# Two heads on alternate partitions: one transpose and one masked copy for both head groups

## The chip, the cores and the metric

The kernel runs on one core of a Trainium2 chip. The metric is the device time of one execution in microseconds. A core has TensorE (PE, matmuls, with its weight loads shown as PEld), VectorE (DVE), ScalarE (ACT), GpSimd (POOL), the queue that issues stores (SP) and 16 DMA engines. PE reads SBUF and writes PSUM.

## The reference

Inputs q, k, v are float32 of shape 8 x 8 x 576 x 64 (batch, head, token, width). The first half is attention inside chunks of 64 tokens, the second mixes the tokens of a batch:

```python
scores = 1/sqrt(64) * q_c @ k_c.T          # per chunk of 64 tokens
attn   = softmax(scores)
x      = (attn @ v_c), heads side by side  # 8 x 576 x 512
wq, wk = x @ w_q, x @ w_k                  # 576 x 64 each
mixed  = 1/sqrt(64) * (wq @ wk.T) @ x
out    = relu(mixed) @ w_out               # 576 x 512, float32
```

## The kernel before

**Order.** The whole program is a list of words, ORDER (L18), one for each step; the loop at L404 turns each into instructions. Each engine takes its own instructions in the order of the list, and semaphores join the engines. A word names the step, the batch, a part, and where it matters a PSUM bank (`@4`) or the engine that does the copy (`:A` ACT, `:D` DVE, `:P` POOL). All work of the eight batches is interleaved in that list; there is no loop over batches.

**Loads.** LD (L115) loads a batch with POOL's DMA queue, which casts float32 to float16 on the way. q and k come in two transfers each, one for each group of four heads (g = 0, 1): partition (head, run) holds a run of 18 tokens, so 4 heads x 32 runs fill 128 partitions, with 18 x 64 elements in each (L137). v comes in four transfers to 32 partitions each (L117). CP (L144) moves half of v 32 partitions up, so that pairs of chunks stand under one another; POOL does it 27 times.

**Transposes.** TR (L172) turns q or k of one head group with DVE, in blocks of 32 x 32 words. A word is two float16 values (the pair of widths 2d, 2d+1). From a block, 32 partitions with the runs of one head, each partition afterwards holds the width pair, and the tokens lie along it as "x r": the 32 values of one block come to stand 18 words apart in q, 9 words apart in k, whose tokens are also split into two halves `e`. q goes to qT, k to kN.

**Masked copies.** The two heads that share 64 rows are kept apart by zeros. MK (L182) copies kN to kT, multiplied by a column `mask` that is 1 on the rows of one head (hp = 0 or 1) and 0 on the others, with separate instructions for even and odd chunks (5 and 4 of them): 2 groups x 2 heads x 2 = 8 instructions a batch.

**Scores to output.** SC (L192) multiplies kT as weights with qT, two matmuls for each pair of words (the even and the odd width, `e`), on the upper and the lower 64 rows at once; both operands are read with a step of 2 float16. EX (L206) takes the exponential on ACT, PV (L220) multiplies with v and a column of ones, RN (L251) divides on DVE. XT and XE (L262, L270) transpose the result on PE and copy it out of PSUM, PJ and EP (L277, L299) give wq and wk, DU (L302) puts a second copy of wq on the other rows, WT and EW (L305, L313) transpose wk, GM and EG (L320, L334) build G = wk.T @ x, MX and RL (L337, L349) multiply wq with G and take the relu, OM and OE (L374, L386) multiply with w_out and copy to the staging tile, which lies over the q and k of batches already used. Stores go through SP's queue; the first two wait until the last two loads have landed (L476).

**Zeros.** ZZ (L400) is a matmul of zeros, 128 x 128 x 512, whose result nobody reads. The order has 48 of them, all but one before the work of batch 2.

Of the kernel before, what the change touches and what calls it, by code (L numbers as in the profile page):

```python
# [23 lines left out]
XE0.0:A RN0.2 XT0.1@0 XE0.1:A ZZ@4 ZZ@5 ZZ@2 ZZ@3 ZZ@6 ZZ@4 PJ0@0 EP0:A TR1.1 TR1.0 MK1.0:D MK1.1:D SC1.0@4 WT0@0
EX1.0 TR1.3 EW0:D TR2.0 CL3 DU0:D TR1.2 MK1.2:A GM0@0 ZZ@7 ZZ@2 PV1.0@2 RN1.0 EG0:A MX0.2@0 MX0.3@6 MK1.3:A RL0.2:A
RL0.3:A TR2.1 MK2.1:D SC1.1@4 EX1.1 SC1.2@0 MX0.0@6 RL0.0:A ZZ@2 ZZ@3 ZZ@2 MX0.1@2 EX1.2 RL0.1:A PV1.1@4 PV1.2@0 ZZ@6
RN1.1 MK2.0:A OM1@6 XT1.0@7 RN1.2 OM2@4 XT1.1@0 XE1.0:D TR2.3 MK2.2:D MK2.3:D TR2.2 LD3.k0 LD3.k1 CP2.0:P LD3.v0
LD3.v1 LD4.k0 CP2.2:P LD3.q1 LD3.v2 LD4.k1 LD3.v3 CP3.0:P CP3.1:P LD4.v0 LD4.q1 LD4.q0 LD5.k0 CP3.2:P LD4.v2 LD4.v1
CP3.3:P SC2.0@2 OM0@7 OE1:A CP2.1:A XE1.1:A EX2.0 OE2:A PJ1@0 PV2.0@2 RN2.0 CP2.3:D TR3.0 EP1:A WT1@6 SC2.1@0 SC2.2@4
DU1:A EW1:A EX2.1 GM1@6 PV2.1@0 RN2.1 EX2.2 EG1:A OE0:A MX1.0@4 MX1.1@2 RL1.0:A RL1.1:A MX1.3@6 PV2.2@4 MX1.2@0  # L30
RL1.3:A RL1.2:A TR3.1 RN2.2 OM4@2 OM6@3 XT2.0@0 MK3.0:A XT2.1@4 TR3.3 MK3.1:D MK3.3:D MK3.2:D TR4.1 ZZ@6 TR3.2 OM5@1
SC3.0@6 OE4:A XE2.0:A XE2.1:A OE5:A EX3.0 PJ2@4 EP2:A OE6:A OM8@1 WT2@0 SC3.1@4 SC3.2@2 OE8:A EW2:A EX3.1 PV3.0@6
EX3.2 GM2@0 PV3.1@4 EG2:A MK4.1:A MK4.0:D TR4.3 RN3.0 OM7@2 OE7:A RN3.1 DU2:P LD5.q0 CP4.0:P LD4.v3 PV3.2@6 MX2.2@0
RL2.2:A MX2.1@4 RL2.1:A MK4.2:D RN3.2 TR4.0 MK4.3:D TR5.1 TR4.2 XT3.0@3 XE3.0:A MX2.0@0 OM3@2 RL2.0:A MX2.3@6 RL2.3:A
XT3.1@4 XE3.1:A LD5.q1 LD5.v1 LD5.k1 LD6.q0 LD5.v3 CP4.1:P CP4.2:P LD5.v0 CP4.3:P LD5.v2 CP5.1:P LD6.k0 LD6.v1 LD6.v3
LD6.k1 LD7.v0 LD6.v2 LD6.q1 LD6.v0 CP5.0:P CP5.2:P CP5.3:P LD7.k0 SC4.0@0 OM9@3 PJ3@4 EX4.0 OE9:A EP3:A OE3:A PV4.0@0
SC4.1@6 EX4.1 WT3@4 OM10@5 SC4.2@2 EW3:A EX4.2 MK5.0:D TR5.0 DU3:D RN4.0 PV4.1@6 RN4.1 GM3@4 PV4.2@0 RN4.2 OM11@2
MK5.1:A EG3:A OE10:A MX3.0@6 MX3.1@3 XT4.0@5 OE11:A RL3.0:A RL3.1:A XT4.1@0 SC5.0@6 MX3.2@2 TR5.3 XE4.0:D MK5.3:D
MK5.2:D TR5.2 XE4.1:A OM13@4 RL3.2:A EX5.0 PJ4@0 MX3.3@2 OM12@5 EP4:A RL3.3:A OE13:A OE12:A SC5.1@0 EX5.1 SC5.2@2
WT4@4 PV5.0@6 EX5.2 EW4:A TR6.0 TR6.1 RN5.0 OM16@5 PV5.1@0 RN5.1 PV5.2@2 GM4@4 RN5.2 OM15@6 XT5.0@7 OE16:A MK6.0:A  # L40
EG4:A MK6.1:D TR6.3 XE5.0:D TR6.2 MK6.3:D MK6.2:D TR7.1 LD7.k1 CP6.1:P LD7.q0 DU4:P LD7.v2 CP7.0:P LD7.v3 CP6.0:P
CP6.3:P LD7.q1 LD7.v1 CP6.2:P MX4.3@4 MX4.1@0 OE15:A RL4.3:A RL4.1:A XT5.1@2 XE5.1:A SC6.0@4 MX4.2@0 OM17@6 EX6.0
PJ5@2 OM14@7 MX4.0@4 OE17:A EP5:A RL4.2:A RL4.0:A WT5@6 EW5:D SC6.1@2 EX6.1 PV6.0@0 SC6.2@4 EX6.2 RN6.0 GM5@6 PV6.1@2
PV6.2@4 RN6.1 RN6.2 DU5:P EG5:A OE14:A MX5.0@0 OM19@6 OM20@7 MK7.1:A RL5.0:A OE19:A OE20:A XT6.0@2 XE6.0:A XT6.1@4
MX5.1@0 RL5.1:A MX5.2@6 TR7.3 XE6.1:D OM18@3 PJ6@4 MK7.3:A EP6:A RL5.2:A OM23@2 TR7.0 MK7.0:D SC7.0@0 WT6@4 MX5.3@6
OE18:A EW6:A CP7.2:P CP7.3:P CP7.1:P DU6:P TR7.2 OE23:D RL5.3:D MK7.2:D EX7.0 OM21@5 GM6@4 PV7.0@0 SC7.2@6 SC7.1@2
OE21:A EG6:A EX7.2 EX7.1 RN7.0 MX6.1@4 OM22@6 RL6.1:D MX6.3@0 PV7.1@2 PV7.2@4 RN7.1 RN7.2 RL6.3:A OE22:A OM26@7
MX6.0@0 OM24@6 RL6.0:A XT7.0@0 XT7.1@4 MX6.2@2 OM25@1 RL6.2:A XE7.0:D XE7.1:D PJ7@4 OM28@0 OE25:A EP7:A WT7@1 OM27@4
# [6 lines left out]
def kernel(  # L55
# [24 lines left out]
    RUN = S // 32  # L80
# [10 lines left out]
    qT = [sb.tile([P, 2, S, 2], F16, name=f"qT{i}") for i in range(2)]  # L91
    kN = sb.tile([P, 2, S, 2], F16, name="kN")
    kT = [sb.tile([P, 2, NCH, 2, CH, 2], F16, name=f"kT{i}") for i in range(2)]
# [21 lines left out]
    def load(b, what):  # L115
        n = int(what[1:]) if what[1:] else -1
        if what[0] == "v":  # L117
            half, f = divmod(n, 2)
            m = slice(NG // 2 * half, NG // 2 * (half + 1))
            src = v[b].rearrange("h (c i e) d -> i (h c) (e d)", i=32, e=2)  # L120
            loads.append(
                nc.gpsimd.dma_start(  # L122
                    vt[b % NVB][CH * f + 32 : CH * f + CH, m, 0 : 2 * D],
                    src[:, NG * half + f : NG * (half + 1) : 2],
                )
            )
            return
        s = "qk".index(what[0])
        if n < 0:
            loads.append(  # L130
                nc.gpsimd.dma_start(
                    qk[b // 2][:, b % 2, s].rearrange("p (g r) d -> p g (r d)", g=2),
                    (q, k)[s][b].rearrange("(g h) (p r) d -> (h p) g (r d)", g=2, r=RUN),
                )
            )
            return
        loads.append(  # L137
            nc.gpsimd.dma_start(  # L138
                qk[b // 2][:, b % 2, s, RUN * n : RUN * n + RUN].rearrange("p r d -> p (r d)"),
                (q, k)[s][b].rearrange("(g h) (p r) d -> g (h p) (r d)", g=2, r=RUN)[n],  # L140
            )
        )

    def pair(b, half, f, eng):  # L144
        m = slice(NG // 2 * half, NG // 2 * (half + 1))
# [24 lines left out]
            )  # L170

    def tr(b, g, s):  # L172
        to = (kN if s else qT[b % 2])[:, g].bitcast(F32).rearrange("p n o -> p (n o)")
        frm = qk[b // 2][:, b % 2, s, RUN * g : RUN * g + RUN].bitcast(F32)
        if s:
            to = to.rearrange("p (e x r) -> p r e x", e=2, r=RUN // 2)
            frm = frm.rearrange("p (r e) x -> p r e x", e=2)
        else:
            to = to.rearrange("p (x r) -> p r x", r=RUN)
        nc.vector.transpose(out=to, in_=frm)  # L180

    def mk(b, g, hp, eng):  # L182
        one = mask[:, hp : hp + 1]
        for odd in range(2):
            dst = kT[b % 2][:, g, odd::2, hp ^ odd].rearrange("p c (e i) o -> p c e (i o)", e=2)
            frm = kN[:, g].rearrange("p (e c i) o -> p c e (i o)", e=2, c=NCH)[:, odd::2]
            if eng == "A":
                nc.scalar.activation(dst, frm, AF.Copy, scale=one)  # L188
            else:
                nc.vector.tensor_scalar(dst, frm, one, None, op0=ALU.mult)  # L190

    def sc(b, u, bank):  # L192
        for i in range(8 if u < 2 else 2):
            g, c = (u, i) if u < 2 else (i, NCH - 1)
            for e in range(2):
                for t in range(2):
                    rows = slice(CH * t, CH * t + CH)
                    nc.tensor.matmul(  # L198
                        ps[:, bank + t, CH * i : CH * i + CH],
                        lhsT=kT[b % 2][rows, g, c, :, :, e].rearrange("p f n -> p (f n)"),  # L200
                        rhs=qT[b % 2][rows, g, CH * c : CH * c + CH, e],
                        start=(e == 0),
                        stop=(e == 1),
                    )
# [199 lines left out]
    for word in ORDER:  # L404
# [107 lines left out]
```

## Time and profile before

| | |
|---|---|
| median of 3 runs | 118.85 us (118.61 to 119.23) |
| profiled execution, its own time | 118.47 us |
| its span, first to last instruction | 116.6 us |
| mean granted clock of PE | 0.985 |

A line of a group view gives line, engine, operation, output and input tile with shape and count, then busy time, mean length of one in ns, and the engine's idle time just ahead of them with what ended it. A line of a timeline gives start, length, engine, line, operation and count; where several instructions are merged, the length is that of the group. One instruction may start while the one before it is in its last stage, so lengths can add up to more than the busy time.

### The profile page before, as it was taken

The numbers are of one execution on the slowest core, as the hardware profiler recorded it, in microseconds if no ns is written. First come the engines' busy times: TensorE is split into PE (matmuls) and PEld (weight loads), VectorE is DVE, ScalarE is ACT, GpSimd is POOL, SyncE is SP. The second block draws the span as 40 slices with busy tenths as digits, with TensorE's granted clock in tenths as the row PEclk, the third lists the DMA queues.
The fourth block names the chain that finished last, engine by engine and source line by source line (L and its number), as shares of the span: only waits on it lengthen the run. The fifth ranks groups of instructions, "written<-read, shape, count | busy, mean of one in ns | idle before, by whom it ended". The sixth has DMA issues, their size and how long they took to land.

```text
span 116.6 us, 4132 instructions
## 1 busy us (share of the span) xinstructions
PE 99.8 (86%) x1768; PEld 55.9 (48%) x1768; DVE 92.4 (79%) x155; ACT 89.5 (77%) x142; POOL 61.9 (53%) x105
## 2 busy tenths in 40 slices
PE   5937998778998799979979979689999979999940
PEld 2403654434665465636644736355654535543410
DVE  2099399999999999999997999998799768515520
ACT  4069907599999999999996998679999982477220
POOL 6958597377679269994769999552500100010000
PEclk9999599999999999999999999999999999999999
DMA  1999999999999999999999999999799986007982
GB/s 11 177 200 177 199 194 211 192 201 203 197 193 204 196 201 186 190 195 194 189 195 165 169 178 200 210 192 129 296 400 415 411 351 280 23 3 304 379 315 88
DMA packets 27202, 24.52 MB, mean 210 GB/s; under 512 B 20784, under 2 KB 20784, under 8 KB 27184
## 3 DMA queue, kind: packets, MB, share of 16 engines
q0 software_dynamic: 24880, 14.82, 90.8%
q1 hardware_dynamic: 2304, 9.44, 20.3%
q8 instruction: 14, 0.23, 0.7%
q14 instruction: 4, 0.03, 0.1%
HBM read 29.62 MB, written 9.44 MB: 335 GB/s over the span
## 4 chain that ended last, share of the span: by engine, by line
DMA 43%; PE 33%; POOL 12%; issue 5%; ACT 2%; DVE 1%; POOLq 0%; DVEq 0%
DMA vt<-in_v_dram 39%; PE pb L378 18%; POOL vt L295 6%; DMA qk<-in_q_dram 4%; POOL vt L122 3%; POOL qk L138 3%; PE pb L341 3%; PE pb L198 3%; PE pb L283 3%; PE pb L266 3%; PE pb L325 2%; PE pb L232 2%; ACT qk L293 1%; DVE xn L255 1%; ACT rmx L356 1%
## 5 line engine op out<-in xcount | busy, mean ns | idle before, releaser
L378 PE MATMUL pb<-wout,rmx 128*128 128x512 f16 x144 | 36.4, 382 | 0.0
L255 DVE TENSOR_TENSOR xn<-pb,rec 128x896 f16<-128x896 f32 (+1 forms) x24 | 25.1, 1047 | 0.8
L295 POOL COPY vt<-vt 32x576 int32<-32x576 int32 x27 | 18.1, 674 | 11.4 <-DMA vt<-in_v_dram 10.7
L122 POOL DMA_DIRECT2D vt<-in_v_dram x32 | 21.8, 687 | 3.4 <-DMA vt<-in_v_dram 1.2
L356 ACT ACTIVATE rmx<-pb 128x576 f16<-128x576 f32 x29 | 18.3, 663 | 5.9 <-PE pb L341 5.7
L180 DVE STREAM_TRANSPOSE kN<-qk 128x576 f32<-128x576 f32 x16 | 19.4, 1213 | 4.0 <-DMA qk<-in_k_dram 4.0
L188 ACT ACTIVATE kT<-kN,mask 128x640 f16<-128x640 f16 (+1 forms) x24 | 17.4, 786 | 5.1 <-DVE kN L180 4.9
L293 ACT COPY qk<-pb 128x512 f32<-128x512 f32 x30 | 17.6, 607 | 4.1 <-PE pb L378 3.9
L180 DVE STREAM_TRANSPOSE qT<-qk 128x576 f32<-128x576 f32 x16 | 19.7, 1243 | 0.1
L208 ACT ACTIVATE est<-pb 128x1024 f16<-128x1024 f32 (+1 forms) x24 | 19.2, 826 | 0.4 <-PE pb L198 0.3
L378 PEld LDWEIGHTS <-rmx 128*128 128x128 f16 x144 | 12.5, 103 | 13.0 <-issue 0.5
L198 PE MATMUL pb<-qT,kT 64*128 64x64 f16 x576 | 13.0, 193 | 4.0 <-ACT kT L188 2.8
L401 PE MATMUL pb<-zz 128*128 128x512 f16 x48 | 14.5, 437 | 1.2 <-DVE zz L423 1.2
L190 DVE TENSOR_SCALAR kT<-kN,mask 128x640 f16<-128x640 f16 (+1 forms) x40 | 14.9, 423 | 0.1
L198 PEld LDWEIGHTS <-kT 64*128 64x128 f16 x576 | 10.8, 96 | 8.1 <-ACT kT L188 4.2
L293 ACT COPY xT<-pb 128x1280 f16<-128x1280 f16 (+1 forms) x10 | 11.4, 1146 | 4.0 <-PE pb L266 3.7
L295 POOL COPY wq<-wqk 64x288 int32<-64x288 int32 x5 | 2.1, 422 | 22.6 <-ACT wqk L293 19.1
L232 PE MATMUL pb<-vt,est 64*64 64x65 f16 x576 | 9.9, 197 | 2.4 <-issue 1.8
L266 PE MATMUL pb<-ident,xn 128*128 128x128 f16 (+1 forms) x160 | 10.9, 214 | 0.4 <-DVE xn L255 0.4
L266 PEld LDWEIGHTS <-xn 128*128 128x128 f16 (+1 forms) x160 | 9.2, 97 | 3.9 <-issue 1.2
L232 PEld LDWEIGHTS <-est 64*64 64x64 f16 x576 | 7.8, 109 | 6.4 <-issue 5.0
L138 POOL DMA_DIRECT2D qk<-in_k_dram x16 | 9.2, 576 | 2.5 <-DMA qk<-in_k_dram 1.1
(40 smaller groups left out, 102.9 us busy)
## 6 DMA issues: line engine op xcount, KB each, us to landing
out_dram<-qk SPq DMA_DIRECT2D x10, 768.0 KB, 6.7
qk<-in_k_dram POOLq DMA_DIRECT2D x16, 288.0 KB, 8.0
qk<-in_q_dram POOLq DMA_DIRECT2D x16, 288.0 KB, 7.9
vt<-in_v_dram POOLq DMA_DIRECT2D x32, 144.0 KB, 7.8
out_dram<-qk SPq DMA_DIRECT2D x6, 256.0 KB, 3.4
wout<-in_moe_w_out_dram POOLq DMA_DIRECT2D x1, 512.0 KB, 9.8
wpj<-in_moe_w_q_dram POOLq DMA_DIRECT2D x1, 64.0 KB, 8.3
wpj<-in_moe_w_k_dram POOLq DMA_DIRECT2D x1, 64.0 KB, 7.6
```

Of the source, the lines that this page charges most:

```text
L122: nc.gpsimd.dma_start(vt[b % NVB][CH * f + 32 : CH * f + CH, m, 0 : 2 * D], src[:, NG * half + f : NG * (half + 1) : 2],)
L180: nc.vector.transpose(out=to, in_=frm)
L188: nc.scalar.activation(dst, frm, AF.Copy, scale=one)
L198: nc.tensor.matmul(ps[:, bank + t, CH * i : CH * i + CH], lhsT=kT[b % 2][rows, g, c, :, :, e].rearrange("p f n -> p (f n)"), rhs=qT[b % 2] ...
L208: nc.scalar.activation(est[b % 2][u].rearrange("p i n c -> p i (n c)"), ps[:, bank : bank + 2, 0:n], AF.Exp, scale=scale_attn,)
L232: nc.tensor.matmul(ps[CH * o : CH * o + CH, bank + hp, VP * m : VP * m + VP], lhsT=est[b % 2][t][rows, i, at], rhs=vt[b % NVB][rows, slot, ...
L255: nc.vector.tensor_tensor(out=xn[b % 2][:, 7 * u : 7 * u + n].rearrange("p m (h d) -> p h m d", h=2), in0=xw[:, :, :, 0:D], in1=rec[u][:, ...
L266: nc.tensor.transpose(t16[:, at % 1024 : at % 1024 + r], xn[b % 2][0:r, n, :], ident[0:r, 0:r])
L293: nc.scalar.copy(dst, src)
L295: nc.gpsimd.tensor_copy(dst.bitcast(I32), src.bitcast(I32))
L356: nc.scalar.activation(dst, src, AF.Relu, scale=scale_moe)
L378: nc.tensor.matmul(ps[:, bank, :], lhsT=c.rearrange("p (t r) -> p r t", r=size)[:, r], rhs=wout[:, i, :], start=(i == 0), stop=(i == NI - 1),)
```

## The change

From batch 1 on, a transfer of q or k still carries one head group, but puts it on every second partition (64 of 128), each with a run of 36 tokens: the two groups then lie on alternate partitions. Batch 0 stays as it was.

One transpose takes both groups. A block of 32 partitions now holds 16 runs of one head from each group, and the two groups' words become neighbours: the tokens lie as "x r g". One masked copy then takes both groups, and even and odd chunks together. For that, kN gets 64 more token places, zeroed once, and kT is laid out in ten chunks of 128 x 2. Scores from batch 1 on read weights and moving side with a step of 4 float16 (2 for batch 0). The last chunk of GM reads 128 rows, of which the upper 64 meet zero weights, and not 64.

The order is a new one. In words that count here: ZZ 48 to 1, TR 32 to 18, MK 32 to 18 (and one instruction for each, not two), MK on ACT 12 to 4 and on DVE 20 to 14; CP on POOL 27 to 22, on ACT 2 to 1, on DVE 3 to 9; DU on POOL 5 to 0, on ACT 1 to 4, on DVE 2 to 4; EP and EG on DVE 0 to 2 each; the second XE on DVE 2 to 4; OE on DVE 6 to 7, RL 3 to 4. The loads of batch 0 start k, k, q, q and not k, q, k, q.

```diff
-            return
-        loads.append(
-            nc.gpsimd.dma_start(
-                qk[b // 2][:, b % 2, s, RUN * n : RUN * n + RUN].rearrange("p r d -> p (r d)"),
-                (q, k)[s][b].rearrange("(g h) (p r) d -> g (h p) (r d)", g=2, r=RUN)[n],
-            )
-        )
+        src = (q, k)[s][b]
+        if b == 0:
+
+            dst = qk[0][:, 0, s, RUN * n : RUN * n + RUN]
+            src = src.rearrange("(g h) (p r) d -> g (h p) (r d)", g=2, r=RUN)[n]
+        else:
+
+            dst = qk[b // 2][n::2, b % 2, s]
+            src = src.rearrange("(g h) (p r) d -> g (h p) (r d)", g=2, r=NG)[n]
+        loads.append(nc.gpsimd.dma_start(dst.rearrange("p r d -> p (r d)"), src))
...
+        elif s:
+            to = to.rearrange("p (e n) -> p e n", e=2)[:, :, 0:S]
+            to = to.rearrange("p e (x r g) -> p r e x g", r=RUN, g=2)
+            frm = frm.rearrange("p (r e) (x g) -> p r e x g", e=2, g=2)
+        else:
+            to = to.rearrange("p (x r g) -> p r x g", r=NG, g=2)
+            frm = frm.rearrange("p r (x g) -> p r x g", g=2)
         nc.vector.transpose(out=to, in_=frm)
...
-        for odd in range(2):
-            dst = kT[b % 2][:, g, odd::2, hp ^ odd].rearrange("p c (e i) o -> p c e (i o)", e=2)
-            frm = kN[:, g].rearrange("p (e c i) o -> p c e (i o)", e=2, c=NCH)[:, odd::2]
...
+        dst = dst.rearrange("p (m j e i) o -> p m j e (i o)", j=4, e=2, i=n)
+        dst = dst[:, :, 1:3] if hp else dst[:, :, 0::3]
+        frm = frm.rearrange("p (e m j i) o -> p m j e (i o)", e=2, j=2, i=n)
...
-                        lhsT=kT[b % 2][rows, g, c, :, :, e].rearrange("p f n -> p (f n)"),
-                        rhs=qT[b % 2][rows, g, CH * c : CH * c + CH, e],
+                        lhsT=kv[rows, g, c, :, e],
+                        rhs=qv[rows, g, CH * c : CH * c + CH, e],
...
-                r = P if j < 4 else CH
...
-                    lhsT=wkn[b % 2][0:r, j, :],
-                    rhs=xn[b % 2][0:r, n, :],
+                    lhsT=wkn[b % 2][:, j, :],
+                    rhs=xn[b % 2][:, n, :],
...
+            pad = kN.bitcast(F32).rearrange("p (e n) o -> p e (n o)", e=4)
+            nc.vector.memset(pad[:, :, S // 2 :], 0.0)
```

More of the change, by code (lines that the diff above doesn't have):

```diff
@@ L24 @@
[L24 to L48, printed above, removed]
@@ L90 @@
     vt = [sb.tile([P, NG, VW], F16, name=f"vt{i}") for i in range(NVB)]
-    qT = [sb.tile([P, 2, S, 2], F16, name=f"qT{i}") for i in range(2)]
-    kN = sb.tile([P, 2, S, 2], F16, name="kN")
-    kT = [sb.tile([P, 2, NCH, 2, CH, 2], F16, name=f"kT{i}") for i in range(2)]
+    qT = [sb.tile([P, 2 * S, 2], F16, name=f"qT{i}") for i in range(2)]
+    SP = S + CH
+    kN = sb.tile([P, 2 * SP, 2], F16, name="kN")
+    kT = [sb.tile([P, 4 * SP, 2], F16, name=f"kT{i}") for i in range(2)]
     mask = sb.tile([P, 2], F32, name="mask")
@@ L183, in mk @@
         one = mask[:, hp : hp + 1]
[L184 to L192 removed]
+        dst, frm, n = kT[b % 2], kN, CH
+        if b == 0:
+            dst, frm, n = dst[:, 2 * SP * g : 2 * SP * g + 2 * SP], frm[:, SP * g : SP * g + SP], CH // 2
+        dst = dst.rearrange("p (m j e i) o -> p m j e (i o)", j=4, e=2, i=n)
+        dst = dst[:, :, 1:3] if hp else dst[:, :, 0::3]
+        frm = frm.rearrange("p (e m j i) o -> p m j e (i o)", e=2, j=2, i=n)
+        if eng == "A":
+            nc.scalar.activation(dst, frm, AF.Copy, scale=one)
+        else:
+            nc.vector.tensor_scalar(dst, frm, one, None, op0=ALU.mult)
+    def sc(b, u, bank):
+        if b == 0:
+            qv = qT[0].rearrange("p (g n) o -> p g n o", g=2)
+            kv = kT[0].rearrange("p (g c m) o -> p g c m o", g=2, c=NCH + 1)
+        else:
+            qv = qT[b % 2].rearrange("p (n g) o -> p g n o", g=2)
+            kv = kT[b % 2].rearrange("p (c m g) o -> p g c m o", c=NCH + 1, g=2)
         for i in range(8 if u < 2 else 2):
```

58 lines of the change are left out of this document (39 added, 19 removed).

## The prediction

> **What bounds the kernel now.** I read the busy shares first, then a table of stretches (columns: stretch and its length, then busy time and instruction count of PE, PE's weight loads, DVE, ACT and POOL, then granted clock, DMA share and GB/s), then the same table for the zero matmuls alone (PE and weight loads only).
>
> ```profile
> span 116.6 us, 4132 instructions
> PE 99.8 (86%) x1768; PEld 55.9 (48%) x1768; DVE 92.4 (79%) x155; ACT 89.5 (77%) x142; POOL 61.9 (53%) x105
> ```
> ```profile
> 0.00:20.00 20.00, 15.61 (x205) 7.81 (x206) 12.55 (x27) 10.55 (x13) 14.98 (x29) 0.91 1.16 166
> 20.00:30.00 10.00, 8.26 (x188) 4.58 (x186) 9.50 (x18) 8.75 (x15) 6.68 (x12) 1.00 1.37 198
> 30.00:80.00 50.00, 44.74 (x916) 27.10 (x915) 48.75 (x79) 46.44 (x75) 37.03 (x60) 1.00 1.37 192
> 80.00:112.20 32.20, 31.22 (x464) 16.44 (x461) 21.63 (x34) 23.27 (x42) 3.24 (x6) 1.00 0.72 276
> 112.20:116.60 4.40, 0.00 (x0) 0.00 (x0) 0.00 (x0) 0.53 (x1) 0.00 (x0) 1.00 0.45 169
> ```
> ```profile
> 0.00:20.00 20.00, 11.72 (x39) 4.04 (x40) 0.91 1.16 166
> 20.00:30.00 10.00, 2.41 (x9) 0.52 (x7) 1.00 1.37 198
> 30.00:80.00 50.00, 0.39 (x1) 0.10 (x1) 1.00 1.37 192
> 80.00:112.20 32.20, 0.00 (x0) 0.00 (x0) 1.00 0.72 276
> ```
>
> The reader is to see three different kernels in one span. From 30 to 80 us DVE is busy 48.75 of 50 us and ACT 46.44: the vector engines set the pace, and PE idles 5.26 us. From 80 to 112.2 PE is busy 31.22 of 32.2 us, with DVE and ACT a third idle: PE works off what it could not do before. Without the zero matmuls PE has 3.89 + 5.85 + 44.35 + 31.22 = 85.3 us of real work. So of the 112.2 us up to its last matmul, PE has no real work in hand for 16.1 us (before 20), 4.15 (20 to 30), 5.65 (30 to 80) and 1.0 (80 to 112.2). Behind that lie 4.4 us of last copy and store. A gain must come out of the 16.1 or out of the 10.8 us after 20.
>
> The loads seem to be a bound too: the rate of the page stands near 195 GB/s until 80 us. The store queue tells when the last loads have landed, because the first store waits for them; the third row is PE's last product with the values of batch 7.
>
> ```profile
> GB/s 11 177 200 177 199 194 211 192 201 203 197 193 204 196 201 186 190 195 194 189 195 165 169 178 200 210 192 129 296 400 415 411 351 280 23 3 304 379 315 88
> 81.63 31.45 SPq L394 DMA_DIRECT2D out_dram<-qk  x16
> 96.51 0.23 PE L232 MATMUL pb<-vt,est 64*64 64x65 f16 x4
> ```
>
> From that product (96.7) to the end is 19.9 us. With loads done at 81.6, and three to four pair copies of 0.7 us (a row below) and the product behind them, the end could be near 105. The loads leave 7 us of room to the span that I forecast.
>
> **The change, part by part.** *Transposes.* The q and k of a batch from 1 on take 2 transposes of 1,152 words instead of 4 of 576: 28 become 14, batch 0 keeps 4. Each group of 32 writes now goes to 16 pairs of neighbouring words instead of 32 single words, 36 or 72 bytes apart.
>
> ```profile
> L180 DVE STREAM_TRANSPOSE qT<-qk 128x576 f32<-128x576 f32 x16 | 19.7, 1243 | 0.1
> L180 DVE STREAM_TRANSPOSE kN<-qk 128x576 f32<-128x576 f32 x16 | 19.4, 1213 | 4.0 <-DMA qk<-in_k_dram 4.0
> L255 DVE TENSOR_TENSOR xn<-pb,rec 128x896 f16<-128x896 f32 x16 | 17.5, 1092 | 0.6
> L255 DVE TENSOR_TENSOR xn<-pb,rec 128x768 f16<-128x768 f32 x8 | 7.7, 958 | 0.3
> ```
> ```profile
> 45.39 1.22 DVE L180 STREAM_TRANSPOSE kN<-qk 128x576 f32<-128x576 f32 x1
> 46.45 1.24 DVE L180 STREAM_TRANSPOSE qT<-qk 128x576 f32<-128x576 f32 x1
> 47.53 1.12 DVE L190 TENSOR_SCALAR kT<-kN,mask 128x640 f16<-128x640 f16 x2
> ```
>
> A transpose holds DVE for 1.07 us (start to start), 1.86 ns a word. The two sizes of L255 differ by 134 ns for 128 elements: DVE passes one in 1.05 ns where nothing hinders it. So the new transpose lies between 1,152 x 1.05 + 0.07 = 1.28 us and 2 x 1.07 - 0.07 = 2.07 us (0.07 for a start: half of the 0.15 that 1,092 ns leave over 896 x 1.05, as neighbours overlap); no transpose of the trace writes neighbours. k (36 bytes apart) and q (72) differ by 30 ns for the same words, so where the writes go does count, and the reads, which are contiguous in both, do not explain the 1.86. I take 1.28. Then the transposes hold DVE for 4 x 1.07 + 14 x 1.28 = 22.2 instead of 34.2 us (-12.0); at 2.07 it would be -0.9.
>
> The Trainium skill (SBUF — State Buffer, "Specifications (TRN2)") has 16-byte lines and asks for two accesses a line for full bandwidth: pairs would pass at full rate, single words not, so by it the sum is the one below. No run here shows it.
>
> *Mask copies.* From batch 1 on 2 instructions per batch with 2,560 elements, in batch 0 4 with 1,280: 18 in all, for 64. DVE gets 12 long and 2 short ones, ACT 2 and 2.
>
> ```profile
> L190 DVE TENSOR_SCALAR kT<-kN,mask 128x640 f16<-128x640 f16 x20 | 8.8, 441 | 0.1
> L190 DVE TENSOR_SCALAR kT<-kN,mask 128x512 f16<-128x512 f16 x20 | 8.1, 406 | 0.0
> L188 ACT ACTIVATE kT<-kN,mask 128x640 f16<-128x640 f16 x12 | 10.1, 844 | 5.1 <-DVE kN L180 4.9
> L188 ACT ACTIVATE kT<-kN,mask 128x512 f16<-128x512 f16 x12 | 8.7, 727 | 0.0
> 65.91 2.50 DVE L190 TENSOR_SCALAR kT<-kN,mask 128x640 f16<-128x640 f16 x4
> 66.17 2.09 POOL L295 COPY vt<-vt 32x576 int32<-32x576 int32 x3
> ```
>
> By the slope of the two sizes (0.273 and 0.914 ns an element) a long one takes 0.97 us on DVE and 2.60 on ACT, a short one 0.62 and 1.43. DVE: 12.8 for 16.9 (-4.1). ACT: 8.1 for 18.8 (-10.7). Beside POOL copies four masks took 2.42 us instead of 1.7: were each long one to wait for one such copy (0.7), DVE would lose 8 us. The means hold such waits already, so I add none.
>
> *What the new order moves.* Counted in the two orders, DVE gets 6 more pair copies, 2 duplicates, 2 projection copies, 2 G copies, 2 xT copies of 1,280, one output copy and one relu.
>
> ```profile
> L297 DVE COPY vt<-vt 32x1152 f16<-32x1152 f16 x3 | 1.4, 453 | 0.7 <-DMA vt<-in_v_dram 0.6
> L297 DVE COPY wq<-wqk 64x576 f16<-64x576 f16 x2 | 0.6, 302 | 0.0
> L358 DVE TENSOR_SCALAR rmx<-pb 128x576 f16<-128x576 f32 x3 | 2.3, 751 | 0.1
> L297 DVE COPY wkn<-pb 128x320 f16<-128x320 f16 x3 | 1.0, 326 | 2.9 <-PE pb L309 2.4 <-ACT rmx L356 0.4
> L297 DVE COPY xT<-pb 128x1280 f16<-128x1280 f16 x2 | 1.6, 812 | 0.0
> L297 DVE COPY qk<-pb 128x512 f32<-128x512 f32 x6 | 4.1, 689 | 4.1 <-PE pb L378 4.1
> ```
>
> 6 x 0.45 + 2 x 0.30 + 2 x 0.75 + 2 x 0.4 (between 0.33 and 0.75) + 2 x 0.81 + 0.69 + 0.75 = +8.7 us, some 3 of it after 80 us where DVE is idle a third. Together DVE goes from 92.4 to 85 (96 with slow transposes). ACT falls to 78.8 by its masks; the xT, projection, G, output and relu copies that DVE takes from it outweigh three more duplicates, so under 79. POOL loses 5 pair copies and 5 duplicates, and its 67 issues stay. The q and k loads past POOL's queue become 64 rows of twice the length; the v loads of the trace fill 32 partitions only and run in the same band of GB/s, so I count no loss.
>
> A new memset of 128 words stands ahead of the first transpose, where DVE waits for its load; without that cover it would cost some 0.1 to 0.2 us.
>
> ```profile
> 5.69 1.21 DVE L180 STREAM_TRANSPOSE kN<-qk 128x576 f32<-128x576 f32 x1 [3.80 <-DMA qk<-in_k_dram]
> ```
>
> *PE.* 47 of 48 zero matmuls go. They lay in time in which PE waited anyway, save part of the 2.41 us after 20; real work stays 85.3, plus 0.3 for the zero that is left. Score reads step 8 bytes instead of 4, in weights and moving side: between nothing and a doubling of 19.5 ns (40 in 0.78 us, below) for 504 matmuls, 9.8 us; I take nothing, since all their reads step already and the nearest change is by one factor of two. G's last chunk reads 128 rows instead of 64 with the same columns: nothing.
>
> *The start.* With the zero matmuls the granted clock was 1.00 but for one stretch:
>
> ```profile
> 10.00:15.00 5.00, 5.00 (x126) 2.77 (x120) 2.92 (x7) 4.46 (x6) 3.51 (x6) 0.66 1.57 193
> 12.16 1.25 PE L198 MATMUL pb<-qT,kT 64*128 64x64 f16 x40
> 47.74 0.78 PE L198 MATMUL pb<-qT,kT 64*128 64x64 f16 x40
> 20.51 1.14 PE L283 MATMUL pb<-xT,wpj 128*128 128x512 f16 x8
> ```
>
> At a clock of 0.66 scores took 1.25 us instead of 0.78, 1.6 times. Without zeros batch 0's steps up to the projection run like that: of 3.2 us on the path (first products, last transposes, projection, next scores) some 1.9 more. k's second half is loaded ahead of q's first, and the first scores come up to 1 us later; two transposes for batch 1 instead of four gain about as much. I take +1.5, between 0 and 3.
>
> **The sum.** Real work 85.6; idle before 20 us 16.1 + 1.5; idle after 20; tail 4.4. The idle after 20 was 10.8. In 30 to 80 us the longest engine was 97.5% busy (48.75 of 50) with the second at 93%; with DVE and ACT shortened PE is the longest there. Kept at 97.5%, its 44.35 us cost 1.1 of idle; at worst 5.65 stays. In 20 to 30 it is 0.3 to 4.15. I take 2.3 and 1.3, nearer the low ends by the 97.5%, and 1.0 after 80: 4.6. Span: 85.6 + 17.6 + 4.6 + 4.4 = 112.2. The profiled execution took 118.47 us, 1.9 above its span, and the median of the runs is 118.85, 0.4 above it: 112.2 + 1.9 + 0.4 = 114.5.
>
> **Rivals.**
> *Transposes stay slow.* The 1.86 ns may belong to the 32 x 32 blocks and not to the writes. For it: no row of neighbouring writes, and the 36- and 72-byte rows differ by 2% only. Then DVE, full from 30 to 80 already, has 96 instead of 92.4: 118.85 + 3.6, about 122.5. It decides from 1.8 us a transpose, where DVE is back at 92.4. Slower; 0.18.
> *The room isn't used.* PE idles 10.8 after 20 us as now, since the new order starves it elsewhere: span 118.4, time 120.7. Against it: the waits of 30 to 80 lie with full DVE and ACT. 0.12.
> *Score reads cost.* Half of the bound of 9.8: 119.4. 0.05.
> *The clock stays low.* If it holds at 0.66 until 30 us, the 5.85 us of work of 20 to 30 takes 1.6 times, 3.5 more: 118. The Trainium skill (TensorE: Matmul & The Clock Gate, "Part 1: The HAM clock gate") has half rate after an idle window of about 3.4 us and full rate after a busy one, which would end this soon after PE is dense; the trace agrees in that the clock is at 1.00 from 15 us on. Faster by a little; 0.05.
> *Everything fits.* Idle at 2.4 after 20, start at no cost: 110.8. 0.12.
>
> **Chances.** Forecast 0.48 (112 to 117.5 as its own range). Within 0.5% (118.3 to 119.4, about what a measurement can tell from no change) only one case falls. Faster: forecast, everything fits and the low clock, 0.65. Within: the score reads, 0.05. Slower: slow transposes and unused room, 0.30. The range takes in everything fits below and the unused room above, 110 to 121.5, and leaves out most of the slow transposes.
>
> **What would show it.** Transposes from batch 1 at 1.2 to 1.4 us each (over 1.8: the first rival); long masks near 0.97 on DVE; DVE's busy time near 85 and ACT's under 79; PE above 95% from 30 us on; 40 scores still in 0.78 us at full clock; clock under 1 before 20 us. The forecast is wrong if PE keeps gaps of 1 us behind DVE or the loads after 30 us, or if the loads land after 89.

## The result and the profile after

| | before | changed |
|---|---|---|
| median of the runs | 118.73 us (118.37 to 119.23) | 150.24 us (149.34 to 150.66) |
| ratio, 95% interval | | 1.264 (1.256 to 1.272) |
| profiled execution's span | 116.6 us | 147.8 us |
| busy PE / DVE / ACT / POOL | 99.8 / 92.4 / 89.5 / 61.9 us | 98.4 / 94.3 / 79.4 / 56.3 us |

The forecast was 114.5 us in a range of 110 to 121.5. The change costs 31.5 us. Medians, here and below, are of all runs of a kernel, ratios of its faster state alone, and the profiles of before_alt_loads, before_split_alt, before_split_adjacent, k_as_before and q_late_and_zeros are of runs in the slower state.

Three lines of the changed kernel's page, the busy times, the granted clock in tenths and the GB/s of 40 equal slices (3.7 us each), and four rows of its table of stretches (columns as in the prediction):

```profile
PE 98.4 (67%) x1721; PEld 61.7 (42%) x1721; DVE 94.3 (64%) x132; ACT 79.4 (54%) x116; POOL 56.3 (38%) x95
...
PEclk9999999999999999975796599999999999999998
...
GB/s 37 194 186 197 208 153 206 213 182 42 4 0 4 0 138 196 193 214 206 181 199 206 206 182 186 143 146 175 407 372 147 217 0 214 3 4 124 372 331 236
```
```profile
0.00:20.00 20.00, 0.00 (x0) 0.00 (x0) 0.92 (x11) 1.28 (x1) 15.43 (x30) 1.00 1.13 163
...
30.00:80.00 50.00, 35.21 (x635) 22.98 (x630) 32.77 (x44) 28.53 (x40) 21.49 (x36) 0.92 0.85 124
80.00:112.00 32.00, 27.48 (x513) 17.72 (x513) 31.50 (x38) 22.67 (x34) 13.44 (x21) 0.92 1.12 232
112.00:147.80 35.80, 32.07 (x437) 17.60 (x435) 21.34 (x32) 21.91 (x37) 0.00 (x0) 0.99 0.40 158
```

No engine got more work than the span can hold: none is busy for over 67%. PE, with 15.6 us in the first 20 before (3.9 of it real work), has nothing there; from 30 to 80 us no engine is over 71% busy, where DVE had 97.5%; and the loads, level near 195 GB/s before, all but stop from 33 to 52 us. So the time went into waiting. The list of waits (us in total, times, longest) and the timelines of DVE, POOL and the store queue (start, duration, and in brackets the idle time before and who ended it) say for what:

```profile
DVE kN L186 <- DMA qk<-in_q_dram: 31.7, 3, 18.6
PE pb L214 <- DVE qT L186: 28.3, 5, 25.2
ACT kT L198 <- DVE kN L186: 25.5, 3, 20.0
PEld L214 <- ACT kT L198: 24.7, 1, 24.7
POOL qk L135 <- DVE qT L186: 23.1, 1, 23.1
```
```profile
20.80 2.23 DVE L186 STREAM_TRANSPOSE kN<-qk 128x576 f32<-128x576 f32 x2 [18.61 <-DMA qk<-in_q_dram]
...
60.61 1.38 DVE L186 STREAM_TRANSPOSE kN<-qk 128x1152 f32<-128x1152 f32 x1 [2.91 <-DMA qk<-in_q_dram]
...
79.76 1.38 DVE L186 STREAM_TRANSPOSE kN<-qk 128x1152 f32<-128x1152 f32 x1 [10.13 <-DMA qk<-in_q_dram]
```
```profile
51.13 0.55 POOL L135 DMA_DIRECT2D qk<-in_q_dram  x1 [23.06 <-DVE qT L186]
```
```profile
101.38 43.86 SPq L409 DMA_DIRECT2D out_dram<-qk  x16
```

The first transpose, of batch 0's **k**, starts at 20.80 instead of 5.69 us, and what ended its wait is a load of **q**. Batch 0's own loads were issued first and are not changed; a transpose of k reads no q. The load of q at 51.13 stood in POOL's queue for 23 us behind a transpose of another batch. With it all later loads stood, so that the first store, which waits for the last loads, comes at 101.4 instead of 81.6. The semaphores of the built programs say the same. The first two transposes of k in DVE's program, of the changed kernel and then of before (a load adds 16 to its semaphore in these programs, and the number is the count waited for):

```
L186 StreamTranspose kN<-qk [waits DMASW4_49 32, DMASW5_49 32, DMASW3_49 32, DMASW0_49 32]
L186 StreamTranspose kN<-qk [waits DMASW1_49 16]

L180 StreamTranspose kN<-qk [waits DMASW0_49 16]
L180 StreamTranspose kN<-qk [waits DMASW2_49 16]
```

In before each waits for its own load alone. In the changed kernel the first waits for all four q and k loads of batch 1, which shares batch 0's tile `qk[0]`: DMASW4 and 5 at 32 are its two loads of q, DMASW3 at 32 is one of k, and DMASW0 reaches 16 with the transpose's own load and 32 with the other load of k. So the new loads, written to `qk[b // 2][n::2, b % 2, s]`, make the dependence tracking of the program order whole tiles: batch against batch, and q against k.

The other rows that the prediction named, all from the changed kernel: groups by form (busy, mean ns), and single rows of the timelines.

```profile
L200 DVE TENSOR_SCALAR kT<-kN,mask 128x2560 f16<-128x2560 f16 x12 | 18.1, 1532 | 0.1
L186 DVE STREAM_TRANSPOSE kN<-qk 128x1152 f32<-128x1152 f32 x7 | 9.6, 1373 | 13.1 <-DMA qk<-in_q_dram 13.0
L186 DVE STREAM_TRANSPOSE qT<-qk 128x1152 f32<-128x1152 f32 x7 | 9.5, 1359 | 0.0
```
```profile
31.45 2.47 PE L282 MATMUL pb<-ident,xn 128*128 128x128 f16 x20 [1.29 <-DVE xn L271]
...
34.93 2.08 PE L299 MATMUL pb<-xT,wpj 128*128 128x512 f16 x8 [0.47 <-DMA vt<-in_v_dram]
...
116.21 1.41 PE L214 MATMUL pb<-qT,kT 64*128 64x64 f16 x40 [0.19 <-DVE kT L200]
...
120.89 1.16 PE L214 MATMUL pb<-qT,kT 64*128 64x64 f16 x32
```

Transposes do what was forecast; long masks are 1.53 us long, and 40 scores take 1.41 us at full clock where before had 0.78. The first two rows are batch 0's transposes and projection at half rate (1.14 us for the projection before), though the page's clock row shows 9 at 31 us: it is no proof of full speed ahead of its first change.

### The profile page after: what moved, and what is told of

It reads as the page before. It is cut to its first block, busy times and chain, and to the rows that moved or that the text cites. A ratio compares the mean times of both kernels' runs of the same rounds, so it can differ in the third digit from the quotient of the medians.

```text
span 147.8 us, 3976 instructions
## 1 busy us (share of the span) xinstructions
PE 98.4 (67%) x1721; PEld 61.7 (42%) x1721; DVE 94.3 (64%) x132; ACT 79.4 (54%) x116; POOL 56.3 (38%) x95
## 4 chain that ended last, share of the span: by engine, by line
PE 30%; DVE 28%; DMA 21%; issue 9%; POOL 8%; ACT 1%; DVEq 0%; POOLq 0%
PE pb L393 14%; DMA qk<-in_q_dram 13%; DVE kT L200 9%; DMA vt<-in_v_dram 8%; PE pb L214 6%; DVE kN L186 5%; DVE qT L186 5%; DVE xn L271 5%; POOL vt L119 3%; POOL qk L135 3%; PE pb L340 3%; PE pb L282 2%; PE pb L248 2%; PE pb L356 2%; DVE xT L313 2%
## 5 line engine op out<-in xcount | busy, mean ns | idle before, releaser
L214 PE MATMUL pb<-qT,kT 64*128 64x64 f16 x576 | 20.6, 238 | 33.2 <-DVE qT L186 28.3
L214 PEld LDWEIGHTS <-kT 64*128 64x128 f16 x576 | 18.2, 118 | 35.4 <-ACT kT L198 24.7
L186 DVE STREAM_TRANSPOSE kN<-qk 128x1152 f32<-128x1152 f32 (+1 forms) x9 | 11.8, 1333 | 31.7 <-DMA qk<-in_q_dram 31.7
L393 PEld LDWEIGHTS <-rmx 128*128 128x128 f16 x144 | 13.4, 106 | 22.4 <-issue 10.5
L309 ACT COPY qk<-pb 128x512 f32<-128x512 f32 x29 | 16.9, 592 | 9.5 <-PE pb L393 9.5
L198 ACT ACTIVATE kT<-kN,mask 128x1280 f16<-128x1280 f16 (+1 forms) x4 | 7.5, 1891 | 25.5 <-DVE kN L186 25.5
L311 POOL COPY vt<-vt 32x576 int32<-32x576 int32 x22 | 14.8, 682 | 14.3 <-DMA vt<-in_v_dram 13.7
L200 DVE TENSOR_SCALAR kT<-kN,mask 128x2560 f16<-128x2560 f16 (+1 forms) x14 | 19.7, 1434 | 0.1
L135 POOL DMA_DIRECT2D qk<-in_q_dram x16 | 8.9, 557 | 26.9 <-DVE qT L186 23.1
L186 DVE STREAM_TRANSPOSE qT<-qk 128x1152 f32<-128x1152 f32 (+1 forms) x9 | 12.0, 1331 | 0.0
L309 ACT COPY xT<-pb 128x1024 f16<-128x1024 f16 (+1 forms) x8 | 8.9, 1121 | 5.4 <-PE pb L282 5.4
L299 PE MATMUL pb<-xT,wpj 128*128 128x512 f16 x64 | 10.1, 305 | 0.5 <-DMA vt<-in_v_dram 0.5
```

Of the source, the lines that this page charges most:

```text
L135: loads.append(nc.gpsimd.dma_start(dst.rearrange("p r d -> p (r d)"), src))
L214: nc.tensor.matmul(ps[:, bank + t, CH * i : CH * i + CH], lhsT=kv[rows, g, c, :, e], rhs=qv[rows, g, CH * c : CH * c + CH, e], start=(e == 0),
L309: nc.scalar.copy(dst, src)
L393: nc.tensor.matmul(ps[:, bank, :], lhsT=c.rearrange("p (t r) -> p r t", r=size)[:, r], rhs=wout[:, i, :], start=(i == 0), stop=(i == NI - 1),)
```

## The experiments

Three theories: **W**, the waits of the stepped loads; **P**, the new steps themselves (score reads, masks); **O**, the new order. Times are medians; a ratio is to before measured beside it (117.5 to 118.1 us).

**The loads alone, in the kernel before.** Loads of q and k of batches 1 to 7 on every second partition, with two runs of 18 tokens each, so that all else stays; two loads of k go ahead of the transposes that now need them.

```diff
-    qk[b // 2][:, b % 2, s, RUN * n : RUN * n + RUN].rearrange("p r d -> p (r d)"),
-    (q, k)[s][b].rearrange("(g h) (p r) d -> g (h p) (r d)", g=2, r=RUN)[n],
+    qk[b // 2][n::2, b % 2, s].rearrange("p (g r) d -> p g (r d)", g=2),
+    (q, k)[s][b].rearrange("(g h) (p r) d -> (h p) g (r d)", g=2, r=RUN)[n::2],
```


> The kernel before, with one part of the change: from batch 1 on the two transfers of q and of k go to the even and to the odd partitions (64 rows of two runs of 18 tokens), still into the tile that two batches share; layout in SBUF, transposes, masks, scores and order stay, but for two loads put ahead of the transposes that now need them. Theory W (waits): the program makes a transpose wait for the other batch's stepped loads into the same tile, and a stepped load wait for the other batch's transposes, so the time rises by most of the 31.5 us: 135 to 150, the second transpose starts behind a load of batch 1 (about 15 to 20 us), and the loads pause once. Theory P (the new steps themselves cost: score reads at 33.6 instead of 19 ns, masks of 1.5 us): nothing of that is in this kernel, 118 to 121.

171.1 us, ratio 1.450 (1.438 to 1.462). The timeline of its POOL:

```profile
51.05 1.22 POOL L106 DMA_DIRECT2D qk<-in_k_dram  x2 [20.68 <-DVE qT L155]
...
120.75 0.62 POOL L106 DMA_DIRECT2D qk<-in_k_dram  x1 [16.86 <-DVE qT L155]
```

Loads of k wait 20.7 and 16.9 us for transposes of q. The change of the loads alone costs more than the whole change: W, though by more than the 135 to 150 us that it expected.

**The changed kernel with tiles that are not shared.** First a tile for each batch, then one for q and one for k of each batch. Output rows are staged in the same bytes, in smaller groups, and the row that straddled two batches gets a tile of its own; the zero matmul is cut to 256 columns to make room.

```diff
-    qk = [sb.tile([P, 2, 2, NG, D], F16, name=f"qk{i}") for i in range(B // 2)]
+    qk = [sb.tile([P, 2, NG, D], F16, name=f"qk{i}") for i in range(B)]        # own_tiles
+    qk = [[sb.tile([P, NG, D], F16, name=f"qk{i}_{s}") for s in range(2)] for i in range(B)]  # split_tiles
+    mid = [sb.tile([P, DM], F32, name=f"mid{i}") for i in range(3)]
```


> The changed kernel with q and k of each batch in a tile of its own (the staged rows that would straddle two tiles get a place of their own, so five stores for a pair of batches and not three; the one zero matmul is half as wide). Nothing else differs. Theory W: the first transpose starts near 6 us again, the loads do not pause, and what is left is the forecast of 114.5 plus 7 us of slower score reads and some of the slower masks: 119 to 126. Theory P: little changes, above 140.

127.6 us, ratio 1.085 (1.078 to 1.091), 1.6 us above W's expectation. One wait of the kind was left: batch 1's k, 2.85 us for q.

> The changed kernel with q and k of every batch in a tile each (own_tiles kept q and k of a batch together, and a transpose of k still waited 2.85 us for the load of q), so that no transpose waits for a load that it does not read. Output rows are staged in the same bytes, in groups of 2 and 1 instead of 3. Theory W (what is left over the kernel before is still false waits between loads and transposes): the 2.9 us and what hangs on them go, 118 to 123 us, first transposes of a batch follow their own two loads. Theory P (what is left is the work of the new steps: score matmuls with an 8-byte step 33.6 instead of 19.5 ns, long masked copies 1.46 instead of 0.97 us): PE's and DVE's busy times stay at 98.6 and 94, 125 to 128 us. Theory O (what is left is the new order): as P, 125 to 128 us.

126.8 us, ratio 1.076 (1.070 to 1.082). Each transpose now waits for its own loads alone. From 1.264 to 1.076: 22 us of the 31.5 were these waits. The last step gave only 0.9 us where W wanted more, so W ends here. P and O had asked for this number alike.

**What stepped loads cost without false waits.** Three arrangements of the loads in the kernel before, with split tiles: as they were, stepped, and stepped with the two loads of a tensor next to each other. Its 48 zero matmuls are 256 columns wide here, half as wide as before; the same holds for the two runs of the old order below.

> The kernel before with q and k of every batch in a tile each and output rows staged in groups of 2 and 1, its loads, steps and order untouched: the control of before_split_alt. If the tiles and the staging cost nothing, within 1.5 us of before, 116.5 to 119.5 us; if they explain part of the 133.4 us of before_split_alt, 121 us or more.

120.7 us, ratio 1.026 (1.019 to 1.032): between the two bounds of the expectation. Its table of stretches:

```profile
0.00:20.00 20.00, 12.19 (x207) 8.85 (x208) 12.85 (x27) 10.91 (x13) 14.74 (x29) 0.83 1.15 166
20.00:30.00 10.00, 7.49 (x184) 4.62 (x184) 9.14 (x18) 8.40 (x15) 6.88 (x12) 0.88 1.37 198
```

The clock is 0.83 and 0.88 where before had 0.91 and 1.00; the narrower zeros are the likely cause, but they weren't tried alone. So 120.7 is the base for the next two.

> The kernel before with q and k of every batch in a tile each and the loads of q and k of batches 1 to 7 on every second partition (two runs of 18 tokens, 64 rows), as before_alt_loads had them in the shared tiles, 171.1 us. All else as before, but output rows are staged in groups of 2 and 1. Theory W (not the loads were slow, but the waits that they make between batches and between q and k in a shared tile): 116 to 120 us, no transpose and no load waits for over 2 us on the other. Theory L (a load of 64 partitions in steps of two is slow in itself): 125 us or more, with the loads done after 90 us.

133.4 us, far over W's expectation and in L's range; the first store, behind the last loads, is at 92.3 us, as L wanted too. The GB/s of its page (slices of 3.3 us), and rows of DVE's and POOL's timelines:

```profile
GB/s 21 185 185 185 189 209 193 197 197 194 207 196 203 196 208 137 10 2 58 161 183 177 178 190 195 204 171 127 388 391 399 165 345 126 4 5 144 394 384 23
```

```profile
34.71 1.26 DVE L156 STREAM_TRANSPOSE qT<-qk 128x576 f32<-128x576 f32 x1 [5.51 <-DMA qk<-in_q_dram]
```
```profile
60.37 0.42 POOL L271 COPY wq<-wqk 64x288 int32<-64x288 int32 x1 [11.41 <-issue]
```

But the load rate is 185 to 209 GB/s over the first 50 us, as before. A transpose of one group now needs both loads, and the old order has up to nine others between them (the expectation below has 14, which was miscounted): batch 2's first transpose of q comes at 34.7 instead of 23.0. Behind that POOL sits 11 us at a duplicate that is late too, with the remaining loads behind it.

> As before_split_alt (133.4 us), with the two loads of each tensor of batches 1 to 7 next to each other in POOL's queue; there a transpose of 576 words that needed one of them now needs both, and the second came up to 14 loads later. Theory Q (the place in the queue made the 16 us): DVE's waits for q and k fall from 18.3 to under 8 us and the time to 118 to 125 us. Theory L (a load of 64 partitions in steps of two is slow in itself): 130 us or more, with a lower rate than the 185 to 210 GB/s of before in the first 40 us.

123.8 us, ratio 1.045 (1.034 to 1.056): by the ratios some 2.3 us above its base. Its list of waits:

```profile
DVE kN L156 <- DMA qk<-in_k_dram: 5.4, 4, 4.0
...
DVE qT L156 <- DMA qk<-in_q_dram: 0.9, 1, 0.9
```

Q holds: DVE's waits for q and k fall from 18.3 to 6.3 us (4.4 in the base). The stepped loads are hardly slow in themselves; their place in the queue counts, since nobody can start on half a tensor. What the last 2.3 us are was not tested.

**The order.**

> The kernel before with the new order, joint words split into their two halves: no stepped loads, no wide reads, no long masks, but also no halved transposes; DVE has the 8.7 us of copies that the new order moves to it. Theory W and theory P both have no cause here: 119 to 128, by DVE's load near 101 us. If the new order itself starves the engines, above 135.

129.6 us, ratio 1.100 (1.091 to 1.109), 1.6 us over the expected range.

```profile
PE 96.3 (76%) x1721; PEld 57.7 (45%) x1721; DVE 103.9 (82%) x183; ACT 80.2 (63%) x124; POOL 56.5 (45%) x95
```

DVE is busy 11.5 us longer than before (the prediction's 8.7 for copies and 12 more masks of 0.42 make 13.7). With the old steps the new order is worse by 12 us.

> The changed kernel in own tiles, with the order of before: a joint transpose or masked copy stands where the first of the two stood. If the new order adds to the loss beside the waits, this is faster than the own tiles in the new order; if it is the better order, slower. Theory W: 116 to 126 in both. Theory P: above 140.

146.5 us, in P's range, but no test of the order: two loads of q waited 12.8 and 7.0 us for transposes of k in the same tile.

> As split_tiles, but with the order of before (a joint transpose or masked copy stands where the first of its two stood, two loads of k are put ahead of the transpose that now needs them); with this the order is tested without the false wait of q on k that spoiled own_old_order. Theory O (the new order costs what new_order_old_code showed, about 11 us): 115 to 120 us, at least 5 us under split_tiles. Theory P (the new steps cost it): within 3 us of split_tiles, 122 to 128 us, DVE's busy time 80 to 85 us, since fewer copies stand on DVE in this order, and PE's real work 7 us over that of before.

139.5 us (138.1 to 140.8), where O wanted 115 to 120 and P up to 128. Both missed:

```profile
DVE qT L158 <- DMA qk<-in_q_dram: 10.2, 2, 5.2
...
DVE kN L158 <- DMA qk<-in_k_dram: 8.6, 4, 3.6
```

By its waits it is the case of before_split_alt again: old places of the loads, steps that need both. The new steps run better in the new order (126.8), the old ones in the old (118); either crossed is worse. So these runs don't price the order by itself: the new steps in the old order, with the loads of a tensor next to each other, were not run.

**The masks.** Each masked copy on DVE as two instructions, for even and odd chunks:

```diff
-            nc.vector.tensor_scalar(dst, frm, one, None, op0=ALU.mult)
+            for j in range(2):
+                nc.vector.tensor_scalar(dst[:, :, j], frm[:, :, j], one, None, op0=ALU.mult)
```


> As split_tiles, but each masked copy on DVE as two instructions, one for the even and one for the odd chunks of 64 tokens, so that its pattern has one loop less. Theory P1 (the long masked copy lost DVE's fast mode because of its pattern: 1.46 us start to start against 0.97 by the slope of before): two of 0.55 us take its place, DVE's busy time falls by 3 to 5 us, and the time by 1 to 3 us against split_tiles. Theory P2 (a masked copy of 2,560 elements costs 0.57 ns an element whatever its pattern): two of 0.75 us, nothing gained, within 0.7 us of split_tiles or slower.

122.7 us, ratio 1.042 (1.038 to 1.046), 4.1 us under split_tiles. A row of its timeline, and four of the changed kernel, masks with the instruction that starts behind them:

```profile
30.98 2.18 DVE L202 TENSOR_SCALAR kT<-kN,mask 128x1280 f16<-128x1280 f16 x4
```
```profile
24.95 0.81 DVE L200 TENSOR_SCALAR kT<-kN,mask 128x1280 f16<-128x1280 f16 x1
25.68 1.22 DVE L186 STREAM_TRANSPOSE qT<-qk 128x576 f32<-128x576 f32 x1
34.70 1.53 DVE L200 TENSOR_SCALAR kT<-kN,mask 128x2560 f16<-128x2560 f16 x1
36.16 1.37 DVE L186 STREAM_TRANSPOSE qT<-qk 128x1152 f32<-128x1152 f32 x1
```

Four of 1,280 elements run in 2.18 us, 1.09 for what one long one did in 1.46 start to start: P1. The length isn't the reason: batch 0's masks have 1,280 elements in the joint pattern, and one holds DVE for 0.73 us, the 0.57 ns an element of the long ones. Against split_tiles DVE's busy time fell by 2.6 us, less than P1's 3 to 5, PE's by 1.0, and the time by more than P1's 1 to 3; why it is more was not tested. The Trainium skill (VectorE: DVE Perf Modes, "What auto-detection actually checks") asks for outermost dimensions that are equal or both even for the mode with two ports. In the built program the source's loops of 5 and 2 chunks are joined to one of 10, the target's outermost loop has 5, and after the split both have 5. The runs agree with that, but show only that the split brings the rate back.

**The score reads.** q, then k, back in the layout of before. Of the edit only the lines that read are shown; the loads and transposes, for k the masks too, are those of before as well:

```diff
-            qv = qT[b % 2].rearrange("p (n g) o -> p g n o", g=2)        # q_as_before
+            qv = qT[b % 2].rearrange("p (g n) o -> p g n o", g=2)
...
-            kv = kT[b % 2].rearrange("p (c m g) o -> p g c m o", c=NCH + 1, g=2)   # k_as_before
+            kv = kT[b % 2].rearrange("p (g c m) o -> p g c m o", g=2, c=NCH + 1)
```


> As split_mask_halves (122.7 us), but q of every batch is loaded and transposed as before (two transposes of 576 words into single words), so that the score matmuls read their moving side, q, at a step of 4 bytes again and only their weights, k, at 8. DVE has 7 x (2 x 1.07 - 1.30) = 5.9 us more. Theory M (the 14 ns that a score matmul takes longer are its 64 moving columns, read at an 8-byte step): 64 of them at full clock in about 1.25 instead of 2.16 us, PE's busy time 7 us lower, near 89; time 117 to 121 us, since PE is the longest engine and DVE's 98 us stand close behind. Theory Wt (it is the weights): 64 in 2.16 us as now, PE as now, DVE longer, 123 to 128 us.

> The mirror of q_as_before: k of every batch loaded, transposed and masked as before in two groups, so that the weights of the score matmuls step by 4 bytes and the moving side by 8. DVE has 5.9 us more for transposes and some 1 us more for masks. Theory M (moving side): 64 matmuls in 2.16 us as now, 123 to 129 us. Theory Wt (weights): 64 in about 1.25 us, PE's busy time near 89, 117 to 122 us. If each side costs half, both kernels show about 1.7 us for 64 and PE near 92.

Batch 7's last 32 scores at full clock, in q_as_before and in k_as_before (1.16 us changed), and 32 of batch 7 in before:

```profile
93.07 0.72 PE L223 MATMUL pb<-qT,kT 64*128 64x64 f16 x32
```
```profile
101.27 1.14 PE L224 MATMUL pb<-qT,kT 64*128 64x64 f16 x32
```
```profile
90.06 0.66 PE L198 MATMUL pb<-qT,kT 64*128 64x64 f16 x32
```

The moving side costs it: 14 to 15 ns a matmul for q, at most 2 ns for the weights. M holds for the matmuls, but its time doesn't: 123.6 us (ratio 1.052, 1.047 to 1.058), and 129.1 for k. PE lost 4.5 us of busy time and DVE got as much:

```profile
30.00:80.00 50.00, 42.81 (x859) 26.46 (x857) 48.67 (x71) 39.08 (x60) 30.08 (x49) 0.97 1.29 185
```

DVE is full from 30 to 80 us. To price the reads alone, read4_no_dve_cost changes the step of the reads in split_mask_halves by one line and leaves the tile as it is written, so the scores multiply with the wrong tokens of q; instructions, transfers and waits stay:

```diff
-            qv = qT[b % 2].rearrange("p (n g) o -> p g n o", g=2)
+            qv = qT[b % 2].rearrange("p (g n) o -> p g n o", g=2)
```


> As split_mask_halves (122.7 us), but the score matmuls of batches 1 to 7 read q at a 4-byte step out of the tile that is still written for the 8-byte one: they multiply with the wrong tokens of q, so the scores and all behind them are not the reference's; every instruction, transfer and wait is the same. Theory R (the last 5 us over before are the score reads): PE's busy time falls by 7 to 8 us, 64 scores in 1.45 instead of 2.16 us, and the time to 114.5 to 117.5 us, at or below before, which is where the forecast stood. Theory S (DVE sets the pace and the start is slow, the score reads are covered): 121 to 123 us.

118.3 us, ratio 1.006 (1.001 to 1.010): 4.4 us under split_mask_halves, 0.8 above R's expectation. Its page and one row of its timeline, then the same scores in split_mask_halves:

```profile
span 116.0 us, 4018 instructions
...
PE 89.9 (77%) x1721; PEld 54.9 (47%) x1721; DVE 91.1 (79%) x146; ACT 78.0 (67%) x116; POOL 56.4 (49%) x95
```
```profile
34.41 1.25 PE L216 MATMUL pb<-qT,kT 64*128 64x64 f16 x64 [0.95 <-DVE qT L187]
```
```profile
34.49 2.16 PE L216 MATMUL pb<-qT,kT 64*128 64x64 f16 x64 [0.90 <-DVE qT L187]
```

64 scores take 1.25 us, for 2.16: 14 ns each, on 504 matmuls 7.2 us of PE (its busy time fell by 6.1), of which 4.4 reach the time. R holds nearly, S falls.

**Two tries for a faster version.** q as before in batches 1, 6 and 7 only (the set (1, 6, 7) in the conditions of q_as_before), then 79 zero matmuls more around batch 0:

> As split_mask_halves (122.7 us), but q of batches 1, 6 and 7 alone as before, where the windows show that DVE has room (13.9 of 20 us busy at the start, 22 of 32 at the end) and PE at the end has none; q_as_before did it in all seven batches and gained nothing, with DVE at 48.7 of 50 us in the middle. Theory B (the 14 ns of a score matmul count only where PE sets the pace, and the 0.85 us that DVE pays a batch only where DVE does): 2 x 72 x 14 ns = 2.0 us at the end and up to 1 at the start, 119.5 to 121.5 us. Theory N (PE's score reads are covered anyway): 122 to 124 us.

> As q_late_batches, with 79 zero matmuls of 256 columns put back ahead of and between batch 0's products, as before had 39 of 512 there. Theory C (without them PE runs at half rate until 24 us: 36 scores 1.15 us, transposes of batch 0 2.46 instead of 1.28, projection 2.08 instead of 1.14, and that lies on the path, which I put at 1.5 us, between 0 and 3): those go to their full-rate durations, 1.5 to 3 us less than q_late_batches, 117 to 119.5 us. Theory H (the start waits for DVE, ACT and the loads anyway): within 0.7 us of q_late_batches.

q_late_batches: 122.6 us (ratio 1.043, 1.034 to 1.051), no gain. That is N's number, but N's reason, covered score reads, is against the 4.4 us above. The stretch from 80 us on in split_mask_halves and in q_late_batches:

```profile
80.00:112.00 32.00, 30.21 (x479) 17.49 (x479) 22.26 (x35) 20.82 (x35) 2.65 (x4) 1.00 0.65 237
```
```profile
80.00:112.00 32.00, 28.92 (x490) 16.09 (x486) 23.35 (x36) 21.09 (x36) 3.65 (x6) 1.00 0.71 242
```

PE's work falls by 1.3 us, and its idle time grows by as much. With the zeros (q_late_and_zeros) the ratio is 1.048 (1.041 to 1.055): no gain either, and C falls. Batch 0's steps did run at full rate there, with 36 scores in 0.71 us for 1.14 and the projection in 1.14 for 2.08, but the projection waited for DVE's copy to xT and ended at 21.32 us, 0.3 earlier than without the zeros. No variant with the whole computation beats the kernel before.

## Why the prediction was wrong

| | us | ratio to before | taken away |
|---|---|---|---|
| changed | 150.2 | 1.264 | |
| split_tiles | 126.8 | 1.076 | waits between loads and transposes |
| split_mask_halves | 122.7 | 1.042 | slow pattern of the masks |
| read4_no_dve_cost | 118.3 | 1.006 | 8-byte reads of q |
| forecast | 114.5 | 0.963 | (the rest: last two points below) |

- **The failed step** is "The q and k loads past POOL's queue become 64 rows of twice the length ... so I count no loss". It priced the transfers, and these did not get slower. It named no wait for them, and none of the five rivals did: neither what a load waits for, nor who waits for it, when two of them write one tile in steps. That is some 22 us of the 31.5. "The loads leave 7 us of room" fell with it; the closing condition, loads that land after 89, is what happened (101.4).
- **Score reads at nothing** was mis-sized. The bound of 9.8 us held: 14 ns more a matmul, 7.2 us on PE, 4.4 in the time. "All their reads step already" was no reason: a price that one step doesn't show can come with the next, as 4 to 8 bytes did. The rival had the price about right (half the bound, 4.9) and a chance of 0.05.
- **Long masks at 0.97 us** was mis-sized: 1.46 start to start, 4.1 us in the time. The slope of two sizes was carried over to a pattern with other loops. Of DVE's 94.3 us, forecast 85, the masks are 7: 19.8 us instead of 12.8. On ACT they came near the forecast (2.43 for 2.60), and so did its total, 79.4 for "under 79".
- **Transposes at 1.28 us** was right: 1.30 start to start, and the rival of slow transposes is out. The rule of the Trainium skill (SBUF — State Buffer, "Specifications (TRN2)"), two accesses to a line, agrees here (1,152 words as pairs in 1.30 us, as single words in 2 x 1.07). Read as two being enough on PE too, it would let an 8-byte step pass free, two to a line of 16 bytes; the 14 ns are against that reading.
- **"With DVE and ACT shortened PE is the longest there"**, said of 30 to 80 us, failed too, and stays wrong with all of the above taken out. The stretches of read4_no_dve_cost:

```profile
0.00:20.00 20.00, 6.63 (x167) 5.49 (x167) 13.34 (x31) 8.22 (x8) 15.70 (x30) 1.00 1.14 164
20.00:30.00 10.00, 8.59 (x193) 5.92 (x194) 8.71 (x15) 6.91 (x10) 6.93 (x12) 1.00 1.25 204
30.00:80.00 50.00, 44.44 (x939) 27.71 (x937) 48.82 (x71) 42.04 (x65) 30.95 (x51) 1.00 1.31 189
80.00:112.00 32.00, 30.20 (x428) 15.76 (x425) 20.24 (x33) 20.23 (x35) 2.79 (x5) 1.00 0.78 277
```

  DVE is busy 48.82 of 50 us, as before (48.75), and PE idles 5.56, where the forecast took 2.3 and before had 5.65. The rival of the unused room (0.12) described this stretch. DVE's total is 91.1 us, forecast 85, with 3.4 of the difference in the masks, even as halves (16.2 for 12.8). Part of the room went to the order: the new steps in the old order, with fewer copies and masks on DVE, keep it busy for 80.2 us (split_old_order), in the new order for 94.7 (split_tiles).
- **The idle total** agrees by luck: 22.1 us up to PE's end at 112.0, forecast 22.2. The first 20 us idle 13.4 instead of 17.6, because batch 0's steps at low clock fill them, and what lies behind 30 us idles more. The start itself came as forecast: at 30 us PE has 74.6 us of work left, by the forecast 74.5 (85.6 less the 11.1 that 30 us hold beside 17.6 and 1.3 of idle); at 80 us 30.2, by the forecast 26.8 (74.5 less 47.7; before 31.2). So of the 3.8 us between the forecast span of 112.2 and the 116.0 of this kernel, 3.3 lie between 30 and 80 us, and the start isn't among them.

## What to carry to other kernels

Before pricing a transfer that is moved or reshaped, list what its new form must wait for and who must wait for it, tile by tile: in the built program's semaphores an extra wait is visible before any time is known. Give stepped writes a tile of their own, and put the loads that are needed together next to each other in the queue. A faster layout for the writer can be slower for the reader; price both sides, and by a row with that very step. Compare idle time stretch by stretch: a total can agree while its parts don't, and room that a change frees on an engine is gone if the new order puts other work there.

## What was not expected of the hardware

- A matmul of 64 columns takes 14 ns longer when its moving side is read at 8 instead of 4 bytes a step (64 in 2.16 and 1.25 us); the same step in the weights costs at most 2 ns (32 in 0.72 and 0.66 us).
- A masked copy of 2,560 elements holds DVE for 1.46 us, and two halves of it, even and odd chunks, for 1.09 us together.
- The page's clock row shows full rate from the start of the changed kernel, while 20 transposes at 31 us take 2.47 us, and 1.28 later on.
